# Linear attention plus a gated top-8 MLP on one core: statistics and norms by one rule in every slot, sums of x from slot 5, tile 1's transposes earlier, reciprocals read back in four partition quarters

## The chip, the cores and the metric

One core of one Trainium2 chip runs the whole program. The metric is the device time of one execution in microseconds. The kernel before has a median of 111.35 us over 3 runs (111.32 to 111.84). Engines are named as in the profile: PE (TensorE matmul), PEld (its weight loads), DVE (VectorE), ACT (ScalarE), POOL (GpSimd), SP (SyncE, which here only issues DMAs).

## What is computed

```python
def reference(A_x, A_wqkv, A_wo, B_x, B_w_r, B_w_gate, B_w_up, B_w_down):
    # A_x: 1 x 2048 x 640, wqkv: 640 x 1920, wo: 640 x 640, w_gate, w_up: 640 x 1536, w_down: 1536 x 640
    x = A_x
    xn = _layernorm(x, axis=-1)
    return x + _A_ref(xn, A_wqkv, A_wo) + _B_ref(xn, B_w_r, B_w_gate, B_w_up, B_w_down)

# _A_ref, 32 heads of 20: q, k, v = xn @ wqkv
phi = lambda t: jnp.where(t > 0, t + 1, jnp.exp(t)) + 1e-6
kv = jnp.einsum("bhsd,bhse->bhde", phi(k), v)
z = jnp.einsum("bhsd->bhd", phi(k))
o = einsum(phi(q), kv) / (einsum(phi(q), z) + 1e-6)
return o @ wo

# _B_ref: r = xn @ w_r, the 8 tokens with the largest r
g = _silu(x_sel @ w_gate); u = x_sel @ w_up
y = (g * u) @ w_down * sigmoid(r_sel)
return xn + scatter(y to those 8 rows)
```

The output is therefore x + xn, plus the attention, plus y on 8 rows.

## The kernel before

The 2048 tokens are 16 tiles of 128. **Part 1** is a prologue for tiles 0 and 1 and a loop `for t in range(2, T)`; one pass of it is called slot t here. For its tile a slot multiplies k (10 matmuls, `k_part` L239) and q (25 matmuls, L254), and adds the previous tile to an accumulator xn-transposed times phi(k) (`ga_mm` L265, three matmuls of 512 columns into gaC and gaD). ACT turns k and q into exp and relu (`phi_act` L223, L224), and DVE combines these to phi (`phi_vec` L233: pk for k, pqT for q).

The matmuls need xn with its columns on partitions, xnT. Tiles 0 to 2 are transposed on PE (`tr_tile` L210) and copied out by ACT or DVE (`tr_evict` L216); from tile 3 on a DMA does it, issued by SP right behind the norm (`ln_norm`, L201 and L206). The layer norm of a tile is `ln_stats` on DVE (two `bn_stats` L172, `bn_aggr` L176), then a short chain of one-column operations on POOL (L181, L186, L188, L189: one over the square root, then the mean), then `ln_norm` on DVE. Up to slot 5 a slot takes the statistics of tile t+3, later of tile t+4; up to slot 6 it norms tile t+2, later tile t+3. Slots 5 and 6 hold the step over: half of tile 9's statistics in each, and two norms in slot 6, the second (tile 9) ahead of the phi of k6.

From slot 9 on DVE also adds xn to x in place (`residual` L400), once in each of slots 9 to 11 and four times in slots 12 to 14; `keep` L403 writes four tiles of that sum to the DRAM buffer xcp in each of slots 12 to 15. SP, in order, issues behind each transposing DMA one of the loads of `late_loads` (L379: x, then wg, wu, wd and wv). `small_consts` builds index constants on POOL in slots 3 to 5, and a few of them on DVE in slot 12.

**Part 2** finds the eight tokens, sums pk over the tokens (zp), and goes on with the accumulators (gbA, L562; gbC, L659). The denominators pden give reciprocals rden (32 heads by 512 tokens in each of four partition groups). Four DMAs store them to DRAM, every head repeated five times (rscr, L689), and `rb_load` (L697) reads them back on 128 partitions as rb: the first 512 tokens, the next 512, then 1024. `norm` (L712) multiplies pqT by rb.

**Part 3** folds wv, the accumulator and wo into M, adds y to xcp by an indirect DMA (L804), reads the sum back to x_sb (L809), and makes the output tile by tile: 10 matmuls (L825), for tiles 0 to 11 a copy by ACT and an addition of x_sb by DVE (L851), for the last four an addition straight from the accumulator (L833), and a store.

The order of work on every engine is that of the program text (`manual_schedule`). Accumulators lie in pairs of banks named A, B and C, and single banks D0 and D1; a new user of a name waits until the old contents have been read. Every DMA issued by SP or ACT has one of eight semaphores, and an issue first waits until the semaphore's previous transfer has landed.

Of the kernel before, what the change touches and what calls it, by code (L numbers as in the profile page):

```python
# [8 lines left out]
P = 128  # L9
# [8 lines left out]
C = 8  # L18
# [16 lines left out]
LAST = (0, 320, 512, 640)  # L35

# [11 lines left out]
def kernel(  # L48
# [194 lines left out]
    def k_mm(t, tag="A"):  # L243
        ps = pair(tag, f"k{t}")
        for kc in range(KC):
            for c in range(2):
                k_part(t, ps, kc, c, xnT[:, kc, t * P : (t + 1) * P])
        return ps

    def q_mm(t, tag="B"):  # L250
        ps = pair(tag, f"q{t}")
        for m in range(KC):
            for kc in range(KC):
                nc.tensor.matmul(  # L254
                    ps[:, m * P : (m + 1) * P],
                    lhsT=wq[:, kc, m * P : (m + 1) * P],
                    rhs=xnT[:, kc, t * P : (t + 1) * P],
                    start=(kc == 0 and m in (0, 4)), stop=(kc == KC - 1),
                    skip_group_check=True,
                )  # L260
        return ps
# [66 lines left out]
    ln_half(2, 0)  # L328
# [8 lines left out]
    def small_consts(t):  # L337
# [18 lines left out]
        elif t == 12:  # L356
# [76 lines left out]
    for kc in range(3, KC):  # L433
        k_part(0, kp, kc, 0, xcT[:, kc, :])
    for kc in range(KC):
        k_part(0, kp, kc, 1, xcT[:, kc, :])
    tr1a, tr1b = bank("D1", "tr1a").bitcast(BF16), pair("C", "tr1b").bitcast(BF16)
    tr_tile(1, tr1a, 0, 2)
    tr_evict(1, tr1a, 0, 2, nc.scalar.copy)
    tr_tile(1, tr1b, 2, KC)  # L440
    tr_evict(1, tr1b, 2, KC, nc.vector.tensor_copy)
    ln_half(2, 1)
    ln_aggr(2)
    ln_half(3, 0)
    ln_half(3, 1)
    ker = k_phi(0, kp)
    kp = k_mm(1, "B")
    qp = q_mm(0, "A")
    ln_norm(2)
    ln_aggr(3)  # L450
    tr2 = bank("D1", "tr2").bitcast(BF16)
    tr_tile(2, tr2, 0, KC)
    phi_vec(pk[:, 0, :], ker, False)
    ker = k_phi(1, kp)
    eq0 = phi_act(qp, "q")
    tr_evict(2, tr2, 0, KC, nc.scalar.copy)
    ln_norm(3)
    ln_stats(4)
    phi_vec(pk[:, 1, :], ker, False)
    qp = q_mm(1, "B")  # L460
# [5 lines left out]
    for t in range(2, T):  # L466
# [58 lines left out]
    spread(1, 2, split[:])  # L525

    zp = pair("A", "zp")
# [30 lines left out]
    gbA = pair("B", "gbA")  # L558
# [109 lines left out]
    gu = pair("A", "gu")  # L668
# [25 lines left out]
    def rb_load(a, b, engs=(nc.sync,)):  # L694
        src = rscr[:, a:b].rearrange("(m s) n -> s m n", m=KC)
        for m in range(KC):
            engs[m % len(engs)].dma_start(  # L697
                rb[:, m, a:b], src[:, m, :].unsqueeze(1).to_broadcast([P // 4, 4, b - a])
            )
# [108 lines left out]
    for a, b in ((0, 2), (2, 4), (4, 8), (8, 12), (12, 16)):  # L808
# [94 lines left out]
```

## Time and profile before

| | |
|---|---|
| median of 3 runs | 111.35 us |
| the profiled execution | 111.45 us |
| its span in the profile | 109.7 us, so 1.75 us lie around the span |
| busy: PE, DVE, ACT, POOL | 103.5, 80.1, 67.2, 36.5 us |
| granted clock of PE | 1.00 in every stretch |
| DMA bytes | 25.64 MB, mean 234 GB/s |
| DMA share of the 16 engines in 35.0 to 63.0 us | 1.11 |

The start times in rows of the timeline are microseconds from the start of the span, and the second number is how long the row lasted. In brackets stands how long the engine was idle before it and what ended that. Busy matmuls overlap, so the distance between starts says more than the busy time: ten k matmuls last 1.55 us in a row of the timeline and the next group begins 1.39 us after them.

### The profile page before, as it was taken

To read this page: it belongs to the slowest core of one execution; us is meant where nothing else is said; L and a number is where in the kernel's file an instruction comes from. 1 tells how busy PE (TensorE), PEld (TensorE's weight loads), DVE (VectorE), ACT (ScalarE), POOL (GpSimd) and SP (SyncE) were. 2 spreads that over 40 slices of the span, in tenths; PEclk is the share of its full clock that TensorE was granted. 3 is DMA by queue.
4 is the path that set the end of the run, shared out by engine and by line. 5 is a ranking of instruction groups with operands and counts; after the bars stand their busy time and mean duration, and the time that the engine had idled before them with its cause. 6 is when DMAs were issued, how large, how long until landed. Compare 5 with 4: busy or idle time off the path is not lost.

```text
span 109.7 us, 2960 instructions
## 1 busy us (share of the span) xinstructions
PE 103.5 (94%) x1147; PEld 68.3 (62%) x1147; DVE 80.1 (73%) x202; ACT 67.2 (61%) x121; POOL 36.5 (33%) x82
## 2 busy tenths in 40 slices
PE   6989999999979999999999999999999969999990
PEld 2557866777647766777667644457995535555560
DVE  3889899999949999996999877704038154956580
ACT  4489977677974887778877775277048552555200
POOL 5522386889987775880000000400005000000000
PEclk9999999999999999999999999999999999999999
DMA  3999022894865959999999990766674798899973
GB/s 74 313 355 326 17 60 60 247 106 150 187 182 102 297 154 367 380 364 169 340 362 394 389 369 12 187 239 174 152 224 145 220 293 256 266 325 392 324 254 120
DMA packets 28046, 25.64 MB, mean 234 GB/s; under 512 B 10880, under 2 KB 26112, under 8 KB 28032
## 3 DMA queue, kind: packets, MB, share of 16 engines
q1 hardware_dynamic: 26016, 23.87, 74.3%
q10 hardware_dynamic: 1840, 1.55, 4.7%
q8 instruction: 9, 0.15, 0.5%
q0 software_dynamic: 176, 0.04, 0.5%
q14 instruction: 5, 0.04, 0.2%
HBM read 17.37 MB, written 5.94 MB: 212 GB/s over the span
## 4 chain that ended last, share of the span: by engine, by line
PE 54%; POOL 13%; DMA 13%; DVE 11%; issue 2%; SPq 2%; ACT 1%; DVEq 0%; POOLq 0%; ACTq 0%
PE q L254 12%; PE k L239 11%; PE o L825 10%; DMA rb<-rscr 9%; PE gbA L562 7%; POOL sq L186 5%; PE gaC L265 4%; DMA wk<-in_A_wqkv_dram 4%; DVE st L172 3%; POOL sq L181 2%; SPq L697 2%; POOL sc L188 2%; PE gaD L265 2%; DVE xn L201 2%; PE gu L672 1%
## 5 line engine op out<-in xcount | busy, mean ns | idle before, releaser
L254 PEld LDWEIGHTS <-wq 128*128 128x128 bf16 x400 | 23.5, 98 | 3.4
L254 PE MATMUL q<-xnT,wq 128*128 128x128 bf16 x400 | 25.0, 219 | 0.0
L239 PE MATMUL k<-wk,xnT 128*128 128x512 bf16 (+1 forms) x150 | 23.2, 300 | 0.3 <-ACT xnT L216 0.3
L825 PEld LDWEIGHTS <-pqT 128*128 128x128 bf16 x165 | 12.7, 98 | 10.5 <-DVE pqT L712 1.3
L223 ACT ACTIVATE eq<-q 128x640 bf16<-128x640 f32 x16 | 11.3, 706 | 10.7 <-PE q L254 10.7
L825 PE MATMUL o<-M,pqT 128*128 128x512 bf16 x110 | 16.1, 299 | 1.0 <-DVE pqT L712 1.0
L239 PEld LDWEIGHTS <-xnT 128*128 128x128 bf16 x150 | 11.7, 98 | 7.9 <-ACT xnT L216 0.5
L186 POOL TENSOR_TENSOR sq<-sq,half 128x1 bf16<-128x1 bf16 x16 | 13.9, 866 | 6.5 <-DVE sq L181 3.7
L172 DVE BATCH_NORM_STATS2 st<-x_sb 128x6 f32<-128x320 bf16 x32 | 14.1, 478 | 1.0 <-DMA x_sb<-in_A_x_dram 1.0
L233 DVE SCALAR_TENSOR_TENSOR pk<-ek,rk 128x640 bf16<-128x640 bf16 x16 | 13.2, 823 | 1.2 <-ACT rk L224 0.4
L233 DVE SCALAR_TENSOR_TENSOR pqT<-eq,rq 128x640 bf16<-128x640 bf16 x16 | 13.1, 820 | 0.7 <-ACT rq L224 0.7
L223 ACT ACTIVATE ek<-k 128x640 bf16<-128x640 f32 x15 | 10.5, 703 | 2.1 <-PE k L239 0.6
L224 ACT ACTIVATE rq<-q 128x640 bf16<-128x640 f32 x16 | 11.2, 700 | 0.0
L849 ACT CAST o_all<-o 128x640 bf16<-128x640 f32 x9 | 6.2, 692 | 7.0 <-PE o L825 7.0
L224 ACT ACTIVATE rk<-k 128x640 bf16<-128x640 f32 x15 | 10.5, 698 | 0.0
L265 PE MATMUL gaC<-pk,xn 128*128 128x512 bf16 x32 | 9.5, 377 | 0.8 <-DVE pk L233 0.8
L712 DVE TENSOR_TENSOR pqT<-pqT,rb 128x2560 bf16<-128x2560 bf16 (+2 forms) x6 | 6.1, 1044 | 5.3 <-DMA rb<-rscr 5.3
L201 DVE TENSOR_SCALAR xn<-x_sb,sc 128x640 bf16<-128x640 bf16 (+2 forms) x17 | 6.9, 411 | 2.0 <-POOL sc L189 1.7
L188 POOL TENSOR_TENSOR sc<-sq,neg 128x1 f32<-128x1 bf16 x12 | 7.9, 656 | 0.9
L610 POOL COPY xsT<-xnT 128x5 bf16 x8 | 1.2, 215 | 21.0 <-DVE zc L612 21.0
L562 PE MATMUL gbA<-pk,xn 128*128 128x512 bf16 x32 | 7.4, 380 | 0.0
L400 DVE TENSOR_TENSOR x_sb<-x_sb,xn 128x640 bf16<-128x640 bf16 x16 | 7.3, 485 | 0.0
(164 smaller groups left out, 127.5 us busy)
## 6 DMA issues: line engine op xcount, KB each, us to landing
xcp<-x_sb SPq DMA_DIRECT2D x4, 640.0 KB, 7.3
x_sb<-in_A_x_dram SPq DMA_DIRECT2D x3, 640.0 KB, 4.4
x_sb<-xcp SPq DMA_DIRECT2D x3, 640.0 KB, 8.4
out_dram<-o_all SPq DMA_DIRECT2D x11, 160.0 KB, 5.1
wg<-in_B_w_gate_dram SPq DMA_DIRECT2D x2, 768.0 KB, 7.0
wu<-in_B_w_up_dram SPq DMA_DIRECT2D x2, 768.0 KB, 6.9
rb<-rscr SPq DMA_DIRECT2D x5, 256.0 KB, 5.2
rb<-rscr SPq DMA_DIRECT2D x8, 128.0 KB, 4.8
```

What stands on the lines that cost most here:

```text
L172: nc.vector.bn_stats(out=stat[t][:, h, :], in_=x_sb[:, t, h * HW : (h + 1) * HW])
L186: nc.gpsimd.tensor_tensor(out=sq[:, 1:2], in0=sq[:, 0:1], in1=half[:], op=ALU.pow)
L188: nc.gpsimd.tensor_tensor(out=sc[:, 1:2], in0=sq[:, 1:2], in1=neg1[:], op=ALU.pow)
L201: nc.vector.tensor_scalar(out=xn[:, t, a:b], in0=x_sb[:, t, a:b], scalar1=sc[:, 0:1], scalar2=sc[:, 1:2], op0=ALU.subtract, op1=ALU.mult,)
L223: nc.scalar.activation(e[:], ps[:, 0:D], AF.Exp, scale=scale)
L224: nc.scalar.activation(r[:], ps[:, 0:D], AF.Relu, scale=scale)
L233: nc.vector.scalar_tensor_tensor(out=dst, in0=ea, scalar=1.0, in1=ra, op0=ALU.min, op1=ALU.add)
L239: nc.tensor.matmul(ps[:, a:b], lhsT=lhsT, rhs=wk[:, kc, a:b], start=(kc == 0), stop=(kc == KC - 1))
L254: nc.tensor.matmul(ps[:, m * P : (m + 1) * P], lhsT=wq[:, kc, m * P : (m + 1) * P], rhs=xnT[:, kc, t * P : (t + 1) * P], start=(kc == 0 an ...
L265: nc.tensor.matmul(gaC[:, c * TBLK : (c + 1) * TBLK] if c < 2 else gaD[:], lhsT=xn[:, t, c * P : (c + 1) * P], rhs=pk[:, t, 0:TBLK], start ...
L562: nc.tensor.matmul(gbA[:, (c - 3) * TBLK : (c - 2) * TBLK], lhsT=xn[:, t, c * P : (c + 1) * P], rhs=pk[:, t, 0:TBLK], start=(t == 0), stop ...
L825: nc.tensor.matmul(ps, lhsT=pqT[:, m, t * P : (t + 1) * P], rhs=M[:, m, a:b], start=(m == M_ORDER[0]), stop=(m == M_ORDER[-1]),)
```

## The change

It has nine parts.

1. `ln_half` is no longer called apart from `ln_stats`. In every slot the statistics are those of tile t+3, and the norm is that of tile t+2.
2. In slot 2 the phi of q1 goes behind the phi of k2.
3. `residual` starts in slot 5, with tile t-5 in each of slots 5 to 12; slot 13 adds tiles 8, 9 and 10, slot 14 tiles 11 to 14, slot 15 tile 15.
4. Tile 1's five transposes on PE stand ahead of the last five matmuls of k0 (129 columns each). DVE copies the first two blocks and ACT the other three, where it was the reverse.
5. In the prologue DVE takes the statistics of tiles 2 and 3 in one piece each, both ahead of tile 2's norm.
6. q0 goes to pair C and q1 to pair A, k1 stays in B; from then on k uses B and q uses A, and zp, gbA and gu change names with them. Tile 2's transposes stand inside q1, behind its first five matmuls.
7. The three DVE operations on constants go from slot 12 to a place behind the candidates of part 2.
8. `rb_load` issues four DMAs of 32 partitions (i, i+4, i+8, ...) and all five blocks, where it issued five DMAs of 128 partitions and one block each.
9. x_sb is read back in eight DMAs of two tiles, where it was two of two tiles and three of four.

```diff
+SUMS = {t: ((t - 5,), ()) for t in range(5, 13)}
+SUMS.update({13: ((8,), (9, 10)), 14: ((11,), (12, 13, 14)), 15: ((15,), ())})
...
-    def q_mm(t, tag="B"):
+    def q_mm(t, tag="A", between=None):
         ps = pair(tag, f"q{t}")
         for m in range(KC):
+            if m == 1 and between is not None:
+                between()
...
-    ln_half(2, 0)
...
+    tr1a, tr1b = bank("D1", "tr1a").bitcast(BF16), pair("C", "tr1b").bitcast(BF16)
+    tr_tile(1, tr1a, 0, 2)
+    tr_evict(1, tr1a, 0, 2, nc.vector.tensor_copy)
+    tr_tile(1, tr1b, 2, KC)
+    tr_evict(1, tr1b, 2, KC, nc.scalar.copy)
     for kc in range(KC):
         k_part(0, kp, kc, 1, xcT[:, kc, :])
-    tr1a, tr1b = bank("D1", "tr1a").bitcast(BF16), pair("C", "tr1b").bitcast(BF16)
-    tr_tile(1, tr1a, 0, 2)
-    tr_evict(1, tr1a, 0, 2, nc.scalar.copy)
-    tr_tile(1, tr1b, 2, KC)
-    tr_evict(1, tr1b, 2, KC, nc.vector.tensor_copy)
-    ln_half(2, 1)
-    ln_aggr(2)
-    ln_half(3, 0)
-    ln_half(3, 1)
+    ln_stats(2)
+    ln_stats(3)
     ker = k_phi(0, kp)
-    kp = k_mm(1, "B")
-    qp = q_mm(0, "A")
+    kp = k_mm(1)
+    qp = q_mm(0, "C")
     ln_norm(2)
-    ln_aggr(3)
-    tr2 = bank("D1", "tr2").bitcast(BF16)
-    tr_tile(2, tr2, 0, KC)
     phi_vec(pk[:, 0, :], ker, False)
+    ln_norm(3)
+    ln_stats(4)
     ker = k_phi(1, kp)
     eq0 = phi_act(qp, "q")
+    phi_vec(pk[:, 1, :], ker, False)
+    tr2 = bank("D1", "tr2").bitcast(BF16)
+    qp = q_mm(1, "A", lambda: tr_tile(2, tr2, 0, KC))
     tr_evict(2, tr2, 0, KC, nc.scalar.copy)
-    ln_norm(3)
-    ln_stats(4)
-    phi_vec(pk[:, 1, :], ker, False)
-    qp = q_mm(1, "B")
...
-        if t == 6:
-            ln_half(9, 1)
-            ln_aggr(9)
-        u = t + 3 + (t > 5)
-        if u < T:
-            ln_stats(u)
-        if t == 5:
-            ln_half(9, 0)
-        u = t + 2 + (t > 6)
-        if u < T:
-            ln_norm(u)
-        q_phi(t - 1, qer)
-        if t == 6:
-            ln_norm(9)
+        if t + 3 < T:
+            ln_stats(t + 3)
+        if t + 2 < T:
+            ln_norm(t + 2)
+        if t > 2:
+            q_phi(t - 1, qer)
         ker = k_phi(t, kp, pr)
-        if t > 8:
-            residual(t - 9 if t < 12 else 4 * (t - 12) + 3)
+        for u in SUMS.get(t, ((), ()))[0]:
+            residual(u)
         phi_vec(pk[:, t, :], ker, False)
+        if t == 2:
+            q_phi(t - 1, qer)
         qer = phi_act(qp, "q")
-        if 11 < t < T - 1:
-            for u in range(4 * (t - 12) + 4, 4 * (t - 12) + 7):
-                residual(u)
+        for u in SUMS.get(t, ((), ()))[1]:
+            residual(u)
...
     spread(1, 2, split[:])
+    small_consts(T)
...
-        for m in range(KC):
-            engs[m % len(engs)].dma_start(
-                rb[:, m, a:b], src[:, m, :].unsqueeze(1).to_broadcast([P // 4, 4, b - a])
-            )
+        for i in range(4):
+            engs[i % len(engs)].dma_start(rb[i::4, :, a:b], src)
...
-    for a, b in ((0, 2), (2, 4), (4, 8), (8, 12), (12, 16)):
+    for a, b in [(2 * i, 2 * i + 2) for i in range(T // 2)]:
         nc.sync.dma_start(x_sb[:, a:b, :], xcp_v[:, a:b, :])
```

Three places show how instructions move. The first is DVE in the prologue, from tile 1's norm on (sc_185 is tile 1's scale, st_195 and mv_237 tile 2's statistics, st_244 and mv_291 tile 3's). Before:

```order
L201 TENSOR_SCALAR xn<-x_sb,sc_185 128x384
L172 BN_STATS st_195<-x_sb 128x6
L216 COPY xnT<-tr1b 128x3x128
L172 BN_STATS st_195<-x_sb 128x6
L176 BN_AGGR mv_237<-st_195 128x2
L181 TENSOR_SCALAR sq_240<-mv_237 128x1
L185 CAST sc_239<-mv_237 128x1
L172 BN_STATS st_244<-x_sb 128x6 x2
L199 RECIPROCAL sc_239<-sq_240 128x1
L201 TENSOR_SCALAR xn<-x_sb,sc_239 128x640
L176 BN_AGGR mv_291<-st_244 128x2
```

The same place in the change (tile 3's mean is mv_247 there):

```order
L203 TENSOR_SCALAR xn<-x_sb,sc_185 128x384
L218 COPY xnT<-tr1a 128x2x128
L174 BN_STATS st_234<-x_sb 128x6 x2
L178 BN_AGGR mv_237<-st_234 128x2
L183 TENSOR_SCALAR sq_240<-mv_237 128x1
L187 CAST sc_239<-mv_237 128x1
L174 BN_STATS st_244<-x_sb 128x6 x2
L178 BN_AGGR mv_247<-st_244 128x2
L183 TENSOR_SCALAR sq_250<-mv_247 128x1
L187 CAST sc_249<-mv_247 128x1
L201 RECIPROCAL sc_239<-sq_240 128x1
L203 TENSOR_SCALAR xn<-x_sb,sc_239 128x640
```

The copy of tile 1's transposes now comes ahead of both halves of tile 2's statistics, and tile 3's mean and variance (three operations) ahead of tile 2's norm.

The second place is DVE in slot 6 and the head of slot 7. Before (sc_620 is the scale of tile 8, sc_689 of tile 9, st_695 the statistics of tile 10, st_762 of tile 11):

```order
L172 BN_STATS st_626<-x_sb 128x6
L176 BN_AGGR mv_687<-st_626 128x2
L172 BN_STATS st_695<-x_sb 128x6 x2
L176 BN_AGGR mv_698<-st_695 128x2
L201 TENSOR_SCALAR xn<-x_sb,sc_620 128x640
L233 SCALAR_TENSOR_TENSOR pqT<-eq,rq 128x5x128
L201 TENSOR_SCALAR xn<-x_sb,sc_689 128x640
L233 SCALAR_TENSOR_TENSOR pk<-ek,rk 128x640
L172 BN_STATS st_762<-x_sb 128x6 x2
```

The same place in the change (st_685 and sc_690 belong to tile 9, sc_620 to tile 8, st_751 to tile 10):

```order
L174 BN_STATS st_685<-x_sb 128x6 x2
L178 BN_AGGR mv_688<-st_685 128x2
L203 TENSOR_SCALAR xn<-x_sb,sc_620 128x640
L235 SCALAR_TENSOR_TENSOR pqT<-eq,rq 128x5x128
L403 TENSOR_TENSOR x_sb<-x_sb,xn 128x640
L235 SCALAR_TENSOR_TENSOR pk<-ek,rk 128x640
L174 BN_STATS st_751<-x_sb 128x6 x2
L178 BN_AGGR mv_754<-st_751 128x2
L203 TENSOR_SCALAR xn<-x_sb,sc_690 128x640
```

Tile 9's norm has gone from the place just ahead of slot 6's pk to slot 7, behind that slot's statistics, and a sum of x stands ahead of pk.

The third place is SP in parts 2 and 3 (rscr is the store of the reciprocals, rb their way back). Before:

```order
L689 DMA rscr<-rden 160x1x512 x4
L697 DMA rb<-rscr 128x1x512 x8
L697 DMA rb<-rscr 128x1x1024 x5
L809 DMA x_sb<-xcp 128x2x640 x2
L809 DMA x_sb<-xcp 128x4x640 x3
```

In the change:

```order
L682 DMA rscr<-rden 160x1x512 x4
L690 DMA rb<-rscr 32x5x512 x6
L690 DMA rb<-rscr 32x5x1024 x4
L800 DMA x_sb<-xcp 128x2x640 x8
L843 DMA out_dram<-o_all 128x640 x10
```

SP issues ten reads of reciprocals where it issued thirteen (ACT issues two in both), and eight of x where it issued five.

More of the change, by code (lines that the diff above doesn't have):

```diff
@@ L241, in k_part, with k_mm @@
         )
-    def k_mm(t, tag="A"):
+    def k_mm(t, tag="B"):
         ps = pair(tag, f"k{t}")
@@ L355, in small_consts @@
             nc.gpsimd.tensor_copy(boff[:], prt[0:NTB, 1:2])
-        elif t == 12:
+        elif t == T:
             nc.vector.tensor_reduce(out=used[:], in_=cmask[:], op=ALU.add, axis=AX.X)
@@ L525 @@
     spread(1, 2, split[:])
-    zp = pair("A", "zp")
+    small_consts(T)
+    zp = pair("B", "zp")
     def z_mm(t):
@@ L556 @@
     nc.scalar.copy(GT[:, 2, 0:TBLK], gaD[:])
-    gbA = pair("B", "gbA")
+    gbA = pair("A", "gbA")
     def gb1(t):
@@ L665, in gb2 @@
             )
-    gu = pair("A", "gu")
+    gu = pair("B", "gu")
     for a, w in enumerate((wg, wu)):
```

## The prediction

> **What bounds the kernel now.** I read the busy times by stretch first, then the waits of PE, then the timeline around each of those waits.
>
> ```profile
> 35.00:63.00 28.00, 28.00 (x313) 19.98 (x311) 26.01 (x56) 21.60 (x40) 10.60 (x19) 1.00 1.11 316
> ```
>
> The waits of PE behind the first 5.6 us, in total, count and longest:
>
> ```profile
> PE o L825 <- DVE pqT L712: 1.0, 1, 1.0
> PE gaC L265 <- DVE pk L233: 0.8, 1, 0.8
> PE k L239 <- ACT xnT L216: 0.3, 1, 0.3
> ```
>
> In the row of the stretch (its length, then PE, PEld, DVE, ACT and POOL busy, clock, DMA share, GB/s) PE works all 28.00 us of slots 8 to 15, at clock 1.00, and DVE 26.01 of them. Nothing there can be gained without less PE work, and the change takes none away: PE's instructions are the same, some in another place. So it can win only where PE stands still, and it loses wherever it makes PE stand. Each of the three waits has a place.
>
> ```profile
> 27.27 1.55 PE L239 MATMUL k<-wk,xnT 128*128 128x512 bf16 x10
> 28.66 0.59 PE L265 MATMUL gaC<-pk,xn 128*128 128x512 bf16 x2
> 30.70 1.55 PE L239 MATMUL k<-wk,xnT 128*128 128x512 bf16 x10
> 31.80 0.45 DVE L201 TENSOR_SCALAR xn<-x_sb,sc 128x640 bf16<-128x640 bf16 x1 [1.53 <-POOL sc L189]
> 33.03 0.59 PE L265 MATMUL gaC<-pk,xn 128*128 128x512 bf16 x2 [0.79 <-DVE pk L233]
> ```
>
> A slot is 3.43 us (k6 at 27.27, k7 at 30.70), and the accumulation follows 1.39 us behind the start of k (27.27 to 28.66). In slot 7 it follows 2.33 us behind (30.70 to 33.03): 0.94 us are lost. The cause stands a row higher: DVE sat 1.53 us in slot 6 waiting for POOL's scale of tile 9, with pk of tile 6 queued behind that norm, and PE needs pk.
>
> ```profile
> 6.94 0.69 ACT L216 COPY xnT<-tr 128x640 bf16<-128x640 bf16 x1 [0.20 <-PE tr L210]
> 7.77 0.37 ACT L216 COPY xnT<-tr1a 128x256 bf16<-128x256 bf16 x1
> 8.20 1.56 PE L239 MATMUL k<-wk,xnT 128*128 128x512 bf16 x10 [0.30 <-ACT xnT L216]
> 9.40 0.27 ACT L414 ACTIVATE r_all<-k,sc 128x1 bf16<-128x1 f32 x1
> 9.73 1.56 PE L254 MATMUL q<-xnT,wq 128*128 128x128 bf16 x25
> 12.51 0.70 ACT L216 COPY xnT<-tr 128x640 bf16<-128x640 bf16 x1
> 12.80 0.59 PE L265 MATMUL gaC<-pk,xn 128*128 128x512 bf16 x2
> 13.45 1.55 PE L239 MATMUL k<-wk,xnT 128*128 128x512 bf16 x10
> 16.87 1.55 PE L239 MATMUL k<-wk,xnT 128*128 128x512 bf16 x10
> 18.38 0.59 PE L265 MATMUL gaC<-pk,xn 128*128 128x512 bf16 x2
> ```
>
> In the prologue k1 starts 0.30 late, q0 0.14 late (1.53 behind k1 where 1.39 is the distance; it waits for ACT's last read of k0 in the same pair, 9.40 + 0.27), and in slot 3 the accumulation 0.12 late (1.51 behind k3).
>
> ```profile
> 76.09 1.87 SPq L697 DMA_DIRECT2D rb<-rscr  x3
> 80.67 3.68 SPq L697 DMA_DIRECT2D rb<-rscr  x5
> SPq L697 <- DMA rb<-rscr: 2.0, 1, 2.0
> 83.11 5.47 DMA rb<-rscr
> 86.52 2.88 PE L825 MATMUL o<-M,pqT 128*128 128x512 bf16 x20
> 88.80 1.49 DVE L712 TENSOR_TENSOR pqT<-pqT,rb 128x2560 bf16<-128x2560 bf16 x1 [3.39 <-DMA rb<-rscr]
> 90.35 1.53 PE L825 MATMUL o<-M,pqT 128*128 128x512 bf16 x10 [0.95 <-DVE pqT L712]
> ```
>
> Output tiles 2 and 3 start at 86.52; their row lasts 2.88, and as with k the next group could start 0.16 before its end, at 89.24. Tile 4 begins at 90.35, so 1.11 us are lost. DVE waits 3.39 us there for the second quarter of rb. The SP rows say why it is late: its issues stop for 2.0 us before 80.67, until an earlier rb transfer (ACT's first, whose semaphore is needed again) has landed. The row of 5.47 us, from the chain of waits, is the landing of the last transfer of that quarter, issued at 83.11: 88.6.
>
> **The change part by part.** Durations are the profiled run's: 111.45 us, which is its span of 109.7 and 1.75 around it, 0.10 above the median.
>
> Slot 6 to 7: tile 9's norm moves from ahead of pk6 to slot 7, a slot after its statistics, so POOL's chain is done when DVE comes to it. Minus 0.94. Two things could give it back. POOL's constants of slots 3 to 5 make its scales late by the same amounts as now, but a norm now stands ahead of pk with one slot's notice in all slots; from POOL's rows I get at most 0.3 us of DVE waiting in slot 5, and pk has about 1.1 us to spare (its end 0.3 into the next slot, its reader at 1.39). And DVE's sums start four slots sooner:
>
> ```profile
> 41.93 1.55 PE L239 MATMUL k<-wk,xnT 128*128 128x512 bf16 x10
> 42.19 0.87 DVE L172 BATCH_NORM_STATS2 st<-x_sb 128x6 f32<-128x320 bf16 x2
> 43.22 0.40 DVE L201 TENSOR_SCALAR xn<-x_sb,sc 128x640 bf16<-128x640 bf16 x1
> 45.59 0.88 DVE L172 BATCH_NORM_STATS2 st<-x_sb 128x6 f32<-128x320 bf16 x2
> ```
>
> That is slot 10 before, with the very mix that slots 5 to 12 get: 42.19 to 45.59 is 3.40 us, under the 3.43 of PE. DVE keeps up but hardly recovers: what it is late at slot 5 (about 0.45 us by my count) stays. The sums cost nothing under that cover; without it each would cost about half a microsecond.
>
> Slot 3: the phi of k2 goes ahead of that of q1, 0.74 us earlier, and the 0.12 goes.
>
> Prologue: PE's two waits (0.44) are removed, but ACT, which PE waits for next, gets longer: it copies three blocks of tile 1 and not two. From 0.69 for 640 columns and 0.37 for 256, 384 take 0.48, 0.11 more. So its copy of tile 2 starts at about 12.6 and ends at 13.3, and k2, which needs it, starts at about 13.35 and not 13.45. Minus 0.10; bounds minus 0.44 (ACT never binds) and plus 0.3 (tile 2's norm, now behind three small operations, holds up its transposes inside q1).
>
> Reads of rb: the same bytes and rows per quarter, in four transfers of 160 KB. SP issues two of the first quarter and ACT two. The stop for ACT's first transfer remains, some 0.3 us longer since it carries a quarter more, but now only the last two of the second quarter lie behind its start, where it was four (80.67 to 83.11). The last is issued at about 80.67 + 0.3 + 0.6 to 1.2 (one issue, by the short and long rows) = 81.6 to 82.2, 0.9 to 1.5 earlier; with 5.5 to land, 87.1 to 87.7. To remove the whole 1.11 it must land by 87.7. I take 0.9 of 1.11; bounds 0 and 1.11, since the gain ends where tile 4 follows tile 3.
>
> [...]
>
> Transposes by DMA: here the change adds risk. Tiles 9 to 15 are now normed in slot t for k in slot t+2, a slot later than before, and the load in between stays where it is on SP.
>
> ```profile
> 33.53 0.57 SPq L379 DMA_DIRECT2D wg<-in_B_w_gate_dram  x1
> 34.36 1.20 SPq L206 DMA_TRANSPOSE xnT<-xn  x1
> 35.61 0.61 SPq L379 DMA_DIRECT2D wg<-in_B_w_gate_dram  x1
> 41.45 0.57 SPq L379 DMA_DIRECT2D wu<-in_B_w_up_dram  x1
> 43.65 1.21 SPq L206 DMA_TRANSPOSE xnT<-xn  x1
> xnT<-xn SPq DMA_TRANSPOSE x1, 2.6
> xnT<-xn SPq DMA_TRANSPOSE x1, 6.5
> xnT<-xn SPq DMA_TRANSPOSE x1, 6.2
> xnT<-xn SPq DMA_TRANSPOSE x1, 4.9
> xnT<-xn SPq DMA_TRANSPOSE x1, 6.0
> ```
>
> The last five rows are landings, in us from the issue, of tiles 9, 10, 11, 13 and 15; tile 10 is issued at 34.36, tile 13 at 43.65. In slot 10 the norm ends at 43.62, 1.7 us into the slot; with DVE 0.45 late, 2.15. k two slots later needs the data 6.86 us into the slot, so 4.7 to 5.1 us are allowed. Tile 9, with no large load just ahead, took 2.6; tile 10, 0.8 us behind the issue of a load of wg, 6.5. In the change a transpose comes about 2.2 us behind the previous load's issue (it ends 1.2 after its start, the load follows, the next is 3.43 on), as tile 13's did (41.45 to 43.65): 4.9. So the wait is 0 to 0.2; I take 0.1. Bounds 0 and 3.2 (below).
>
> At no cost: the three constants of slot 12 (some 0.5 us) fall into 0.90 us in which DVE waits for pc; the eight reads of x land in smaller pieces, where DVE waits for the reads now while PE goes on. If these covers go, the constants cost 0.5 and the three more issues, at 0.4 to 0.5 each, up to 1.5 at the end.
>
> Sum: -0.94 - 0.12 - 0.10 - 0.9 + 0.1 = -1.96; 111.45 - 1.96 - 0.10 = 109.4.
>
> **The rivals.** First, the quarters bring nothing: the second quarter lands no sooner, because the 16 engines rather than the issue set the time. For it: four transfers write the same rows; against it the 2.0 us stop. 109.4 + 0.9 = 110.3.
>
> Second, the stall of slot 7 moves and is not removed: the early sums keep DVE behind, and pk or a norm arrives late in some slot from 5 on. For it, 3.40 of 3.43 us; against it, 1.1 us to spare. If 0.94 comes back: 110.3.
>
> Third, slower: the transposes of tiles 10 to 15 land too late, with the loads of wu, wd and wv queued ahead. The place is PE's k, the point is a landing over 5.1 us. At 6.2 a slot pair takes 1.7 + 6.2 = 7.9 us and not 6.86, 0.52 a slot; six slots make 3.2 us: 109.4 + 3.2 = 112.6. For it, three of the four landings quoted of these tiles took 6.0 us or more; against it, the first two came behind two loads issued 2.1 us apart (33.53 and 35.61), which the change spreads over two slots. [...]
>
> **How the numbers follow.** The forecast gets 0.55, the first rival 0.18, the second 0.08, two of the losses together (110.8 to 111.9) 0.10, the third 0.09. Faster by over 0.5%, about what a measurement can tell, means under 110.8: 0.55 + 0.18 + 0.08 = 0.81, taken as 0.80. Within 0.5%: 0.11. Slower: 0.09. The forecast's own range is 108.6 (all of 0.44, 1.11 and no late transpose: 0.34 + 0.21 + 0.1 below) to 110.0. The range goes a tenth below that, and up over the two rivals of 110.3 and most of their pairs, to 111.2; it leaves out the third.
>
> **What would show it.** In the changed profile the wait of the accumulation for pk in slot 7 is gone and slots 4 to 15 start 3.43 us apart; if not, k waiting for a transposing DMA shows the third rival, and DVE's rows behind pk the second. k2 starts near 13.3. Output tile 4 follows tile 3 within 0.3 us, and the last rb read of the second quarter is issued near 82 in the time of before. The prediction is wrong if any slot from 8 on shows PE idle over 0.3 us, or if the end, between the last output matmul and the last store, grows by more than 0.3.

## The result, and the profile after

The changed kernel has a median of 110.92 us over 22 runs (109.22 to 113.55), the kernel before, measured with it, 111.70 (22 runs, 110.33 to 113.99). The ratio is 0.9894, with a 95% interval of 0.9853 to 0.9934; ratios here are formed from the undisturbed runs of a measurement, medians from all of them. The sign and the range of the prediction held; the forecast's own 108.6 to 110.0 us did not. Of the 1.96 us forecast about 1.2 came by the ratio and 0.78 by the medians, and the profiles show that the time was won and lost in other places than the sum had them.

The first profiled execution of the changed kernel is no faster than the one of before: 110.14 us of span against 109.73. Read by stretches, that is no contradiction. The stretches are bounded by the first matmul of k0 and of k2, of k15, of the first output tile (o0) and of the last one. Since one execution turned out to be a poor witness, both kernels were profiled again later (their experiments stand below), and all five are shown here. Two of the three executions of the changed kernel took longer (111.91 and 111.92 us) than the median of their measurement (110.92 and 111.22), so the table tells where time goes and is no measure of the gain.

| us | before | before again | after | after, 2nd | after, 3rd |
|---|---|---|---|---|---|
| start to k0 | 5.61 | 5.64 | 6.83 | 5.61 | 5.94 |
| k0 to k2 | 7.84 | 8.25 | 8.79 | 7.92 | 7.42 |
| k2 to k15 | 45.61 | 45.62 | 44.98 | 45.86 | 45.21 |
| k15 to o0 | 24.61 | 24.61 | 24.63 | 24.63 | 24.62 |
| o0 to last output tile | 21.62 | 20.50 | 20.47 | 20.47 | 20.39 |
| last output tile to the end | 4.43 | 4.46 | 4.43 | 5.71 | 5.28 |
| span | 109.73 | 109.08 | 110.14 | 110.20 | 108.86 |

Between before again and after's third the difference of 0.22 us is 0.53 won up to k2, 0.41 won in the slots, 0.11 at the outputs, and 0.82 lost at the end. The 0.53 are not the change's alone: k0 starts 0.30 later in after's third, and in before again k0 to k2 takes 0.41 more than in the first profile, since the first three matmuls of k0 last 1.22 us there instead of 0.81 (the last section comes back to this).

The first profile of after, timeline (start, length, engine, line, operation; in brackets the idle time before it and what ended that):

```profile
6.83 1.01 PE L241 MATMUL k<-wk,xcT 128*128 128x512 bf16 x3 [1.86 <-DMA wk<-in_A_wqkv_dram]
...
52.86 0.58 SPq L382 DMA_DIRECT2D wd<-in_B_w_down_dram  x1
53.49 0.54 SPq L406 DMA_DIRECT2D xcp<-x_sb  x1
54.21 0.45 DVE L203 TENSOR_SCALAR xn<-x_sb,sc 128x640 bf16<-128x640 bf16 x1 [0.58 <-POOL sc L191]
54.68 2.32 SPq L208 DMA_TRANSPOSE xnT<-xn  x1
...
60.61 1.56 PE L241 MATMUL k<-wk,xnT 128*128 128x512 bf16 x10 [0.27 <-DMA xnT<-xn]
...
88.05 4.24 PE L816 MATMUL o<-M,pqT 128*128 128x512 bf16 x30
```

Three things are to be seen. PE idles 1.86 us until wk has landed, which has nothing to do with the change. The wait of slot 7 is gone, but k15 waits for its transposing DMA, issued at 54.68 behind a load of wd and a copy to xcp: the slot takes 3.86 us instead of 3.43. And output tiles 2, 3 and 4 follow each other without a gap (30 matmuls in one row), where before tile 4 stood 1.11 us for rb.

The late wk costs more than its own time in this execution. The busy time by stretch (length, then PE, PEld, DVE, ACT, POOL busy, granted clock, DMA share, GB/s) shows for the 10 us behind the start, and for a part of them:

```profile
5.60:15.60 10.00, 8.77 (x89) 6.40 (x90) 7.13 (x27) 6.87 (x15) 1.68 (x3) 0.83 0.60 187
7.31:10.72 3.41, 3.41 (x21) 2.13 (x20) 1.02 (x3) 1.51 (x4) 0.00 (x0) 0.50 1.12 335
```

The clock is 0.83 there, since it is 0.50 from 7.31 to 10.72 us, and k0 to k2 takes 8.79 us, where the third profile takes 7.42.

### The profile page after: what moved, and what is told of

The parts are those of the page before. It is cut to its first block, busy times and chain, and to the rows that moved or that the text cites. A ratio compares the mean times of both kernels' runs of the same rounds, so it can differ in the third digit from the quotient of the medians.

```text
span 110.1 us, 2963 instructions
## 1 busy us (share of the span) xinstructions
PE 104.0 (94%) x1147; PEld 68.9 (63%) x1147; DVE 80.4 (73%) x202; ACT 67.3 (61%) x121; POOL 37.7 (34%) x82
## 3 DMA queue, kind: packets, MB, share of 16 engines
HBM read 17.37 MB, written 5.94 MB: 212 GB/s over the span
## 4 chain that ended last, share of the span: by engine, by line
PE 83%; DMA 10%; DVE 1%; ACT 1%; issue 1%; DVEq 0%
PE k L241 19%; PE q L258 18%; PE o L816 14%; PE gbA L555 7%; PE gaC L269 6%; DMA xnT<-xn 5%; DMA wk<-in_A_wqkv_dram 5%; PE gbC L652 4%; PE gaD L269 3%; PE gu L665 1%; DVE o_all L824 1%; PE pkv L728 1%; PE M L763 1%; PE zp L525 1%; PE pden L633 1%; PE o5a L816 1%
## 5 line engine op out<-in xcount | busy, mean ns | idle before, releaser
L188 POOL TENSOR_TENSOR sq<-sq,half 128x1 bf16<-128x1 bf16 x16 | 13.1, 818 | 8.2 <-DVE sq L183 5.7
L190 POOL TENSOR_TENSOR sc<-sq,neg 128x1 f32<-128x1 bf16 x12 | 9.9, 827 | 0.9
L842 DVE TENSOR_TENSOR o_all<-o_all,x_sb 128x640 bf16<-128x640 bf16 x12 | 5.3, 489 | 3.9 <-DMA x_sb<-xcp 2.3
```

Source lines behind the costliest of these rows:

```text
L188: nc.gpsimd.tensor_tensor(out=sq[:, 1:2], in0=sq[:, 0:1], in1=half[:], op=ALU.pow)
L190: nc.gpsimd.tensor_tensor(out=sc[:, 1:2], in0=sq[:, 1:2], in1=neg1[:], op=ALU.pow)
```

## The experiments

Each kernel is described by its difference from another one. Ratios are to the kernel before, measured together with it.

**One part at a time.** First (e1), only the reads of rb by quarters, nothing else:

```diff
-        for m in range(KC):
-            engs[m % len(engs)].dma_start(
-                rb[:, m, a:b], src[:, m, :].unsqueeze(1).to_broadcast([P // 4, 4, b - a]))
+        for i in range(4):
+            engs[i % len(engs)].dma_start(rb[i::4, :, a:b], src)
```

> The kernel before with the reads of rb by four partition quarters alone. Theory (the stop of SP's issues for ACT's first rb transfer made the second quarter late): output tile 0 to the last output tile's first matmul falls from 21.63 us to about 20.5 (20.48 in the changed kernel), all other stretches stay, time 1.0 to 1.2 us (1.0%) lower. Rival (the engines and not the issues set the time, so partition quarters bring nothing): 21.6 us there and the time of before. A second rival (the x reads in eight pieces were needed for it): a part of the 1.1 us comes back as DVE waits at the end.

Measured: median 111.68 us against 111.38, ratio 1.0029 (0.9989 to 1.0069). The quarters alone bring no time. Its profile had a late wk (k0 at 6.82) and has no gap at the outputs (20.39). DVE's products with rb stand in one row there, the one that needs the second quarter last:

```profile
86.80 2.62 DVE L710 TENSOR_TENSOR pqT<-pqT,rb 128x640 bf16<-128x640 bf16 x3
```

DVE does not wait for the second quarter at all, where it waited 3.39 us in the first profile of before. So the quarters do land sooner; the time does not follow.

Second (e2), before with the slot rule: statistics three and norms two tiles ahead, the phi order of slot 2, sums from slot 5.

```diff
-        u = t + 3 + (t > 5)
...
-        u = t + 2 + (t > 6)
...
-        if t == 6:
-            ln_norm(9)
+        if t + 3 < T:
+            ln_stats(t + 3)
+        if t + 2 < T:
+            ln_norm(t + 2)
```

> The kernel before with the slots' rule alone: statistics three and norms two tiles ahead, the phi of q1 behind that of k2, sums from slot 5; the prologue, the constants, rb and x reads as before. Theory: from k2's first to k15's first matmul 45.61 us become 44.99 as in the changed kernel: 0.94 and 0.12 gone, and k15 waits about 0.4 us for tile 15's transposing DMA, issued behind 1280 KB; other stretches as before; time 0.6 us (0.5%) lower. Rival (the wait at k15 came from the disturbed start of the profiled execution): no wait, 44.55 us, 1.06 us lower. Second rival (the transposes are late in more tiles once the start is not late): more than one wait of k for a DMA, 45.5 us or more, no gain.

Measured: median 111.77, ratio 1.0005 (0.9955 to 1.0054), runs from 110.08 to 114.69. Its profile is an execution without any wait in the slots (k2 to k15 44.55 us, thirteen times 3.43), span 108.36. So k15's wait did not come here. It also has no gap at the outputs (20.39), although it reads rb as before does; but the end takes 5.30 us instead of 4.43. PE gained 1.06 us in the slots of that execution, the median nothing; this kernel, too, reads x back in the five old pieces.

Third (e3), before with the new prologue and the names of the pairs that go with it (parts 4 to 6 of the change):

```diff
+    tr_evict(1, tr1a, 0, 2, nc.vector.tensor_copy)
...
+    tr_evict(1, tr1b, 2, KC, nc.scalar.copy)
     for kc in range(KC):
         k_part(0, kp, kc, 1, xcT[:, kc, :])
...
+    qp = q_mm(1, "A", lambda: tr_tile(2, tr2, 0, KC))
+    tr_evict(2, tr2, 0, KC, nc.scalar.copy)
```

> The kernel before with the changed prologue and pair names alone; the slots' rule, sums, constants, rb and x reads as before. Theory (the late start of the changed kernel's profile, k2 at 15.62 us instead of 13.45, is wk landing 1.2 us late and the clock falling, and not the change): with wk landing by 5.5 us k2 starts at about 13.35 us, 0.1 lower, and the time is that of before within 0.3%; when wk is late it is late by as much in either kernel. Rival (the new prologue itself costs, by tile 2's norm or ACT's longer copy): k2 starts at 13.7 us or later with wk on time and the clock at 1.00, time 0.3 us or more higher. Second rival (ACT is not what binds): k2 at about 13.0, 0.4 us lower.

Measured: median 110.70, ratio 0.9936 (0.9896 to 0.9975): this part alone is faster. Its timeline:

```profile
5.97 0.81 PE L241 MATMUL k<-wk,xcT 128*128 128x512 bf16 x3 [0.44 <-DMA wk<-in_A_wqkv_dram]
...
8.20 1.56 PE L241 MATMUL k<-wk,xnT 128*128 128x512 bf16 x10
...
12.38 0.70 ACT L218 COPY xnT<-tr 128x640 bf16<-128x640 bf16 x1
...
13.38 1.55 PE L241 MATMUL k<-wk,xnT 128*128 128x512 bf16 x10
```

k0 to k2 takes 7.41 us against 7.84. ACT's copy of tile 2 is through at 13.08, 0.30 before k2 needs it: ACT does not bind there, and both of PE's waits are won. Here, too, no gap stands at the outputs (20.39) with the old reads of rb.

Multiplied, the three ratios give 0.997, where the whole change has 0.989. Each is known to about 0.4 to 0.5%, so noise may be a part of the difference. Parts 7 and 9 of the change (the constants, the reads of x in eight pieces) ran in no kernel alone, and whether they bring anything is not shown.

Fourth (e4), the changed kernel with the first copy to xcp a slot later, behind the transposing DMA of tile 15:

```diff
+        if t == 13:
+            keep(0, 4)
...
-        if t > 11:
+        if t > 12:
             keep(4 * (t - 12), 4 * (t - 11))
```

> The changed kernel with the first write of four tiles of x to the DRAM buffer issued behind tile 15's transposing DMA instead of ahead of it, nothing else. Theory (that DMA is late because 640 KB of wd and 640 KB of this write are queued ahead of it): its landing falls from 5.9 us to about 4, k15 does not wait, k2 to k15 is 44.55 us instead of 44.99, time 0.4 us lower than the changed kernel, about 1.7 to 2.1 lower than before. Rival (POOL's late scale of tile 15, for which DVE waited 0.58 us, makes it late, not the queue): the landing stays near 5.9 and k15 still waits 0.3 us or more.

Measured: median 110.14, ratio 0.9901 (0.9852 to 0.9950), against the changed kernel's 0.9894 in its own measurement: the ratio is the same, the runs lie closer together (109.25 to 111.36). The profile has 44.55 us in the slots, and 5.41 at the end.

**Both kernels once more.** The kernel before, unchanged (e8):

> The kernel before once more, unchanged, for a second profile of it. Theory 'one execution': the wait of output tile 4 for rb (1.11 us in the first profile) is not there, the stretch from the first output matmul to the last output tile is 20.39 us as in e2 and e3, which read rb as before, and the end is 4.6 to 5.3 us. Rival 'of the kernel': it is 21.3 to 21.7 and the end 4.43. Slots 3 and 7 are as in the first profile (3.55 and 4.37 us; 45.61 from k of tile 2 to k of tile 15).

Its timeline, and SP's waits (us in total, times, longest):

```profile
33.48 0.59 PE L265 MATMUL gaC<-pk,xn 128*128 128x512 bf16 x2 [0.79 <-DVE pk L233]
...
86.96 4.24 PE L825 MATMUL o<-M,pqT 128*128 128x512 bf16 x30
...
87.21 1.49 DVE L712 TENSOR_TENSOR pqT<-pqT,rb 128x2560 bf16<-128x2560 bf16 x1 [1.35 <-DMA rb<-rscr]
```

```profile
SPq L697 <- DMA rb<-rscr: 2.3, 1, 2.3
```

The wait of slot 7 is there again, as are slots of 3.55 and 4.37 us. The gap at the outputs is not: tiles 2 to 4 run in one row from 86.96, although SP's issues of rb stopped for 2.3 us, longer than the 2.0 of the first profile. DVE still waits for the second quarter, but 1.35 us instead of 3.39: its last read landed 3.4 us behind its issue, 5.5 in the first profile. The end takes 4.46 us, not the 4.6 to 5.3 expected.

The changed kernel, unchanged, twice more (e7 and e12):

> The changed kernel once more, unchanged. Theory 'order of the queue': tile 15's transposing DMA lands late whenever SP's first copy of x to xcp and wd are issued right ahead of it, so PE waits 0.2 to 0.5 us before k of tile 15 again and the stretch from k of tile 2 to k of tile 15 is 44.8 to 45.0 us. Rival 'one execution': it is 44.55 as in e2 and e4. On the start: theory 'wk late is of the execution': k's first matmul may stand anywhere from 5.6 to 6.9 us, and where it is 5.7 the way from there to k of tile 2 is 7.41 (clock 1.00), not 8.79. Ratio near 0.990, as first measured.

> The changed kernel once more, beside e11 on the same chip, so that their spreads can be compared. Theory 'lead' (transposing DMAs of tiles 8 to 15 issued 5.1 to 5.9 us ahead, which take 2.6 to 6.3): median 110.3 to 111.2, 0.6 us or more above e11's, highest above 111.5, and if the profiled execution is over 110.5 us long it shows a wait on a transposed tile. Rival 'the spread is of the start and the end': median and spread within 0.3 us of e11's.

Measured: 111.22 us against 111.44 (ratio 0.9861, 0.9798 to 0.9924, formed from only three runs; runs up to 115.18), and 110.63 against 111.09 (0.9922, 0.9884 to 0.9959; runs up to 113.83). The second profile, timeline of SP and PE, and a row of its chain of waits (start, length, what):

```profile
32.35 1.21 SPq L208 DMA_TRANSPOSE xnT<-xn  x1
33.61 0.57 SPq L382 DMA_DIRECT2D wg<-in_B_w_gate_dram  x1
...
35.80 1.21 SPq L208 DMA_TRANSPOSE xnT<-xn  x1
...
37.90 1.56 PE L241 MATMUL k<-wk,xnT 128*128 128x512 bf16 x9 [0.23 <-DMA xnT<-xn]
...
42.12 1.56 PE L241 MATMUL k<-wk,xnT 128*128 128x512 bf16 x10 [0.62 <-DMA xnT<-xn]
```

```profile
35.80 6.27 DMA xnT<-xn
```

And the third:

```profile
45.89 1.21 SPq L208 DMA_TRANSPOSE xnT<-xn  x1
...
51.61 1.56 PE L241 MATMUL k<-wk,xnT 128*128 128x512 bf16 x9 [0.40 <-DMA xnT<-xn]
```

All three profiles of the changed kernel wait for a transposed tile, each mainly for another one: tile 15; tiles 9 and 10; tile 13. (In the second and third k15 comes about 0.1 us late besides.) So it isn't only the copy to xcp ahead of tile 15. The second execution loses 1.31 us of the ideal 44.55, more than the 1.06 that the slots gained. What these tiles have in common is a short lead of the transposing DMA, from its issue to the k that reads it:

| lead in us, tile | 8 | 9 | 10 | 11 | 12 | 13 | 14 | 15 |
|---|---|---|---|---|---|---|---|---|
| before | 5.51 | 6.22 | 7.57 | 8.18 | 8.59 | 8.56 | 8.59 | 9.39 |
| after, first profile | 5.16 | 5.16 | 5.13 | 5.16 | 5.13 | 5.16 | 5.13 | 5.92 |

In the changed kernel landing takes 2.6 to 6.3 us (second profile). A lead of 5.13 leaves no margin for that, 8.5 does. It isn't used up in every execution: the profiles of e2 and e4, and those of e5 and e6 below, have the same leads and no wait (44.55).

**The end.** The first read of x back from xcp has to wait for the indirect DMA that adds y. In the profile of the fourth experiment, timeline of POOL and SP, SP's wait, and the stretches of 2 us:

```profile
82.15 1.75 POOL L797 DMA_INDIRECT xcp<-y_sb,rowu  x1 [12.18 <-DVE y_sb L796]
...
89.14 4.51 SPq L802 DMA_DIRECT2D x_sb<-xcp  x8
...
104.12 1.22 SPq L861 DMA_DIRECT2D out_dram<-o_all  x2
```

```profile
SPq L802 <- DMA xcp<-y_sb,rowu: 5.6, 1, 5.6
```

```profile
84.00:86.00 2.00, 2.00 (x17) 1.10 (x15) 1.43 (x2) 1.30 (x3) 0.00 (x0) 1.00 1.03 307
86.00:88.00 2.00, 2.00 (x16) 1.13 (x15) 0.00 (x0) 0.76 (x2) 0.00 (x0) 1.00 0.54 141
88.00:90.00 2.00, 2.00 (x17) 1.18 (x16) 0.94 (x1) 1.31 (x2) 0.00 (x0) 1.00 0.04 9
```

The add is issued at 82.15 and lets SP go on at 89.14; in the last of the three stretches the 16 engines move next to nothing (share 0.04). From there it is 18.94 us to the end of the span, in e2's kernel 18.98, in after's first profile 19.11. So the next kernel (e5) is e4's without the add, which leaves y's rows out of the sum:

```diff
-    nc.gpsimd.indirect_dma_start(
-        out=xcp[:], out_offset=bass.IndirectOffsetOnAxis(ap=rowu[:, 0:1], axis=0),
-        in_=y_sb[:], in_offset=None, compute_op=ALU.add,
-    )
```

> The kernel of e4 without the indirect DMA that adds y's rows to xcp (the second block's rows are left out of the sum), so the reads of x no longer wait for it and follow SP's last read of rb. Theory 'second bound': with outputs that start without a wait, the end is the later of two things, the first matmul of the last output tile + 4.43 us and the first read of x + about 18.95 us (before 19.69, where the first ends last; after 19.10; e2 18.98 and e4 18.94, where the second ends last). Here the first read of x goes out near 83.5 instead of 89.14, so only the first is left: the stretch from the last output tile's first matmul to the end is 4.4 to 4.6 us instead of e4's 5.41, and the time is about 0.9 us under e4's (near 109.2 us, ratio near 0.982). Rival 'the last stores are slow for a cause of their own': that stretch stays at 5.3 to 5.4 us and the time stays within 0.3 us of e4's.

Its timeline:

```profile
83.47 5.91 SPq L798 DMA_DIRECT2D x_sb<-xcp  x8
92.44 8.63 SPq L841 DMA_DIRECT2D out_dram<-o_all  x10
103.07 0.33 SPq L849 DMA_DIRECT2D out_dram<-o_all  x1
104.82 0.83 SPq L857 DMA_DIRECT2D out_dram<-o_all  x2
```

The reads of x begin at 83.47 and the end takes 4.41 us, 1.00 less than in e4's kernel; from k2 on it is 93.96 us instead of 94.97. The median is 109.93 (4 runs), ratio 0.9867 (0.9800 to 0.9934). So the late start of the reads is what lengthened the end in e4's profile.

Then a kernel (e6), e4's again, that keeps the add and sends it sooner: the product py, its copy to y_sb and the add stand ahead of pkv (moved text, nothing else):

```diff
+    py = pair("A", "py")
...
     pkv = bank("D0", "pkv0"), bank("D1", "pkv1")
...
     norm(0, 1)
 
-    py = pair("A", "py")
```

> The kernel of e4 with the second block's last product py (48 matmuls, 0.83 us of PE), its eviction and the indirect add moved ahead of pkv, that is, 1.58 + 0.56 us earlier on PE; nothing else moves. Theory 'second bound': the add goes out near 80.0 instead of 82.15 and lands up to 2.1 us sooner, near 87.0 to 87.5 (not before the reads of rb are through, near 87); the first read of x follows, the end is then set by PE again, last output tile's first matmul + 4.4 to 4.6, and the time is 0.6 to 0.9 us under e4's (ratio 0.982 to 0.985). Rival 'the add lands when the reads of rb have left the rings': the first read of x stays near 89.1 and the time stays e4's (0.990). Rival 'slow stores': the first read of x comes sooner, the end stays 5.3 to 5.4.

Measured: median 110.64, ratio 0.9935 (0.9897 to 0.9972). The add goes out at 80.54, the first read of x at 85.15, 4 us sooner than in e4's, and the end takes 4.42. But o0 comes 25.44 us behind k15, not 24.63: the end's gain of 0.99 is paid back with 0.81. The waits of ACT and PE there:

```profile
ACT M L793 <- PE M L782: 2.4, 1, 2.4
PE M2a L782 <- DVE kvT L754: 0.3, 1, 0.3
```

I read it so: in its old place py filled PE while DVE and ACT emptied banks; without it ACT sits 2.4 us until M's first chunk (1.1 in e4) and PE waits for kvT. That wait shows 0.3 of the 0.81 us; the rest has no row of its own, so this cause is in part argued.

**More lead for the transposes.** Next (e9), the changed kernel with half of tile 9's statistics at the end of slot 5, the rest and all of tile 10's in slot 6, tile 10's norm at the end of slot 7, and then four and three tiles ahead; sums from slot 9 as before:

```diff
-        if t + 3 < T:
-            ln_stats(t + 3)
-        if t + 2 < T:
-            ln_norm(t + 2)
+        if t == 6:
+            ln_half(9, 1)
+            ln_aggr(9)
+        elif t + 3 + (t > 6) < T:
+            ln_stats(t + 3 + (t > 6))
+        if t + 2 + (t > 7) < T:
+            ln_norm(t + 2 + (t > 7))
...
+        if t == 5:
+            ln_half(9, 0)
+        elif t == 6:
+            ln_stats(10)
+        elif t == 7:
+            ln_norm(10)
```

> The changed kernel with norms three tiles ahead again from slot 8 on, by another way than before: half of tile 9's statistics at the end of slot 5, the other half and tile 10's at the start and end of slot 6, tile 10's norm at the end of slot 7, then statistics four and norms three tiles ahead; sums of x from slot 9 as before. Theory 'lead': the transposing DMAs of tiles 8 to 15 are issued 5.13 to 5.92 us ahead of their k in the changed kernel and take 2.6 to 6.3 us to land in its two profiles, so that some executions wait 0.4 to 1.3 us; with 8.5 us of lead from tile 11 on (tiles 8 and 9 stay at 5.1) none waits: k of tile 2 to k of tile 15 is 44.55, the highest of the timed runs comes down and the median is 109.6 to 110.2 (ratio 0.983 to 0.989). Rival 'DVE has no room': the extra 0.48, 0.69 and 0.39 us of DVE in slots 5 to 8 make phi of k late, a wait of 0.3 to 0.9 us on pk stands in slots 6 to 8, and the ratio is 0.990 or above.

Measured: median 109.66 us (6 runs, 109.30 to 110.91) against 111.25, ratio 0.9889 (0.9830 to 0.9948). The lead is 4.17, 5.77, 7.19, 8.13, 8.33, 8.54 and 8.91 us for tiles 9 to 15, no slot waits (44.55), and the end takes 4.79. It is the lowest median of a full kernel here, but by the ratio it is no better than the changed kernel (0.9894). It was not measured together with the changed kernel, six runs are few for the claim that the spread is narrower, and one profile without a wait, as e2's and e4's with the short lead, does not show that the longer lead ends the waits.

The same (e10), with the last quarter of rb behind the first eight tiles of x and the norm of tiles 12 to 15 behind the first four sums:

```diff
-    rb_load(2 * TBLK, S)
+    rb_load(2 * TBLK, 3 * TBLK)
...
         nc.sync.dma_start(x_sb[:, a:b, :], xcp_v[:, a:b, :])
+        if b == 8:
+            rb_load(3 * TBLK, S)
```

> The kernel of e9 with the last quarter of rb (four reads, 640 KB) issued behind the first 8 tiles of the reads of x instead of ahead of them, and the norm of tiles 12 to 15 behind the sums of the first four output tiles. Theory 'second bound', and 'the add lands when the reads of rb have left the rings': 640 KB less ahead of it, the indirect add lands about 1.7 us sooner (3.7 to 5.3 us after its issue instead of 5.6 to 7.0), the first read of x goes out near 4.8 us after the first output matmul instead of 6.8, the end is last output tile + 4.4 to 4.6 us instead of 5.4, and the time is 0.6 to 1.0 us under e9's (ratio 0.975 to 0.983). Rival 'the add takes its time whatever is ahead of it' (as its 5.6 to 7.0 us): the first read of x stays 6.8 us behind the first output matmul, and e9's time is unchanged. Rival 'the norm comes late': output tile 12 waits for rb, a gap of PE between 0.3 and 2 us near 98, and the time is above e9's.

POOL and SP in its timeline:

```profile
82.60 1.75 POOL L805 DMA_INDIRECT xcp<-y_sb,rowu  x1 [12.17 <-DVE y_sb L804]
...
87.38 1.90 SPq L810 DMA_DIRECT2D x_sb<-xcp  x4
89.33 2.55 SPq L700 DMA_DIRECT2D rb<-rscr  x4
```

The add lets the reads go after 4.78 us instead of 6.64, as expected. The time did not follow: median 110.46, ratio 0.9953 (0.9913 to 0.9994), the end 4.90, no gap at tile 12. From the first matmul of the last output tile to the last DMA packet it is short again (3.16 us; 3.06 in before), but the span ends 1.74 us behind that packet instead of 1.37, and tile 9, with 4.53 us of lead, costs 0.35. Why its median is 0.8 above e9's stays open.

Last (e11), e9's kernel with the norm ahead of the statistics from slot 7 on, to give tiles 9 and 10 more lead:

```diff
+        if t > 6 and t + 2 + (t > 7) < T:
+            ln_norm(t + 2 + (t > 7))
         if t == 6:
...
-        if t + 2 + (t > 7) < T:
-            ln_norm(t + 2 + (t > 7))
+        if t < 7:
+            ln_norm(t + 2)
```

> The kernel of e9 with the norm ahead of the statistics on DVE from slot 7 on, so that each transposing DMA of tiles 9 to 15 is issued 0.9 to 1.2 us sooner: in e9's profile those of tiles 9 and 10 had 4.17 and 5.77 us of lead, the shortest, and e10, which has the same order, waited 0.35 us for tile 9's. Theory 'lead': tile 9 has 5.0 to 5.4 us of lead, tiles 11 to 15 8 to 9.5; k of tile 2 to k of tile 15 is 44.55 and the median 109.4 to 109.9 (ratio 0.982 to 0.988), with no timed run above 111.3. Rival 'the spread is of the start and the end, not of the transposes': the highest of the timed runs stay above 111.5, as the changed kernel's beside it.

```profile
37.35 0.55 POOL L191 TENSOR_TENSOR sc<-sq,neg 128x1 f32<-128x1 bf16 x1
...
37.85 0.18 POOL L192 CAST sc<-mv 128x1 f32<-128x1 bf16 x1
38.07 0.45 DVE L204 TENSOR_SCALAR xn<-x_sb,sc 128x640 bf16<-128x640 bf16 x1 [1.23 <-POOL sc L192]
...
40.39 0.94 PE L242 MATMUL k<-wk,xnT 128*128 128x512 bf16 x4 [1.34 <-ACT rq L227]
```

Measured: 112.89 us, ratio 1.015 (1.011 to 1.019), slower than before, and k2 to k15 47.34 us. Tile 9's lead did grow, to 6.34. But the statistics that used to stand ahead of the norm had been the time in which POOL made its scale; now DVE stands 1.23 us for it, phi comes late behind it, and PE waits 1.34 us. It is the mechanism of slot 7 before, made again in several slots.

## Why the prediction was right, and where it was not

**Slot 7 and slot 3: right.** Minus 0.94 and 0.12 were forecast; the profiles of e2, e4 and e5, in which nothing else waits in the slots, show 44.55 us for k2 to k15 instead of 45.61 and 45.62, which is 1.06. The second rival, that the stall moves on DVE, did not come. That is what the profiles show; the timed runs of e2, which has this part alone, are no faster than before (1.0005).

**Prologue: right in mechanism, mis-sized.** The term was minus 0.10, since ACT's longer copy was to bind. It measures 0.43 (e3: 7.41 against 7.84 in the first profile), the far bound. The same two numbers stand in the other profiles without the long first matmuls of k0 that the last section shows (the first three last 0.81 us in e2, e4, e5 and e11): 7.84 in e2, which has the old prologue, 7.41 or 7.42 in e4, e5, e11 and after's third, which have the new one. ACT's copy of tile 2 ended 0.30 us ahead of its reader, not with it.

**Reads of rb: sooner, as the sum had it, but worth nothing; the second largest term.** The step that failed is "I take 0.9 of 1.11". It prices a gap of PE that only one execution has: before's second profile and those of e2 and e3 read rb in the old way and show 20.39 to 20.50 us for the outputs. The second quarter does land sooner. DVE waits for it 3.39 and 1.35 us in the two profiles of before, and not at all in e1 and in those of the changed kernel. But only the 3.39 reached PE, and SP's stop, the cause that was named, does not make them alone: it is 2.0 us there and 2.3 in the second profile. What differs is the landing of the quarter's last read, 5.5 us against 3.4; why it took so long stays open. The quarters alone measure 1.0029. So the first rival has the time right and the reason wrong, since by it the second quarter lands no sooner.

**Transposes by DMA: mechanism seen, price too low.** The term was plus 0.1, from a landing of 4.9 us; in the changed kernel's three profiles it is 0.43, 1.31 and 0.66 us over the 44.55. The point given for the third rival, a landing over 5.1 us, is the right one (6.27 and 5.68 were measured), but it is passed by two or three tiles of an execution and not by all six, so its 3.2 us did not come either. By the test set down, no slot from 8 on over 0.3 us idle, the forecast fails in the second and third profile (0.62 and 0.40).

**The end: a cover that did not hold.** The eight reads of x were put at no cost because PE goes on meanwhile. In 14 profiles the end is never earlier than the later of two things, the last output tile plus 4.4 us and the first read of x plus 18.9. In the first profile of before PE's is the later by 0.76 us. With the stall of slot 7 gone PE is sooner there, and the reads and stores behind the add come last: by 0.96 us in e4's profile, and by 0.82 in e2's, where x is still read in five pieces, so the eight pieces are not the reason. The end of the changed kernel grew by 1.28 and 0.85 us in its second and third profile, over the 0.3 allowed. The late reads explain only 0.40 and 0.04 of that; both belong to the five of the 14 profiles whose end is 0.2 to 0.9 later than either of the two, which these runs do not explain. In the first profile the end did not grow, since there wk and k15 had made PE late anyway.

So it is partly luck that the time lies in the range: 0.33 us more came from the prologue, none of the 0.9 from rb, and 0.3 to 1.2 more were lost to late transposes and up to 1.3 at the end, more or less by execution. These terms are from single profiles and do not add up to the measured gain: the three spans of the changed kernel have a mean of 109.73 us, the two of before 109.41. What its faster executions do better is not shown by a profile of it.

## What to carry to other kernels

A stall seen in one execution is worth a term only after a second profile of the same kernel shows it too; the one in slot 7 came back to 0.01 us, the one at the outputs did not come back in three further profiles with the old reads. When a stall is removed, ask what else was hidden behind it: here a DMA's lead that fell from 8.5 to 5.1 us against landings of up to 6.3, and a chain of an add, reads and stores that set the end in some of the profiles. Look also at who waits for a transfer before making it faster: the quarters ended DVE's wait for rb, and PE had no use for that. An instruction that stands between a producer and its reader, as the statistics between POOL's scale and the norm or py between M's evictions, may be their cover; move it only with something put in its place.

## What had not been expected of the hardware

The start varies from run to run, whatever the kernel: wk let PE start k0 between 5.61 and 7.50 us. From k0 on the matmuls differ too, and the clock column does not tell all of it. In these traces the record of the granted clock does not begin with the span, and the column shows 1.00 for what has no record. In the first profile of before the record begins at 5.06 us (only from there on is its 1.00 "in every stretch" a measured one), in before again at 6.50, in after's second profile at 6.67, in e1's at 9.88. The first three matmuls of k0 last 0.81 us in the first profile of before, but 1.22, 1.31 and 1.44 in the other three, where k0 starts ahead of the record, at 5.64, 5.61 and 6.82, and k0 to k2 takes 8.25, 7.92 and 9.23 us there. That the clock was lower ahead of its record is my reading of these times. From e1's timeline, and from its busy time by stretch (the clock is the figure behind POOL's), which shows nothing of it:

```profile
6.82 1.44 PE L239 MATMUL k<-wk,xcT 128*128 128x512 bf16 x3 [1.34 <-DMA wk<-in_A_wqkv_dram]
```

```profile
5.60:15.60 10.00, 8.48 (x87) 5.86 (x88) 6.39 (x24) 6.61 (x15) 2.24 (x3) 1.00 0.61 191
```

Behind an idle PE the clock was lower in one of these executions, and in another nothing shows that it was: in after's first profile the record has 1.00 from 3.89 us on, but 0.50 from 7.31 to 10.72, behind an idle 1.86 us; in e11, behind 2.03 us, the first three matmuls of k0 last 0.81 us and k0 to k2 takes 7.41. From e11's timeline, and from its busy time by stretch:

```profile
7.50 0.81 PE L242 MATMUL k<-wk,xcT 128*128 128x512 bf16 x3 [2.03 <-DMA wk<-in_A_wqkv_dram]
```

```profile
5.60:15.60 10.00, 7.99 (x92) 5.92 (x95) 7.38 (x27) 7.71 (x17) 1.97 (x4) 1.00 0.63 199
```

The stretch at 0.50 in after's first profile is 3.41 us long. What decided between the two executions is not shown.

The accumulating indirect DMA landed later where more reads of rb were ahead of it: SP goes on 6.99 us behind its issue in e4's kernel, with twelve such reads, and 4.78 in e10's, with 640 KB fewer ahead of it. The share of 0.04 from 88 to 90 us in e4's kernel does not mean that the reads were through. Between 87.5 and 89.2 us the queue of the reads still moves packets, 14 of them, and the add's queue 9 (queue and kind, packets, MB, share of the 16 engines):

```profile
q1 hardware_dynamic: 14, 0.02, 3.7%
q0 software_dynamic: 9, 0.00, 1.5%
```
